# The first batch's 16-token blocks laid over each other, its zeros written by GpSimd, and the first chunk's PSUM pairs, layouts and conversion pieces put in another order

## The chip, the cores and the metric

The kernel runs on one core of a Trainium2 chip. The core has five engines that each work through a list of instructions in order and wait for one another by semaphores: TensorE (PE in the profile, its weight loads PEld), VectorE (DVE), ScalarE (ACT), GpSimd (POOL) and SyncE (SP), which here only starts transfers. The metric is the device time of one execution in microseconds (us); the median of several executions is compared.

## The reference

Two stages are chained. The first is a delta-rule recurrence over 768 tokens for 4 batches and 8 heads of width 48, the second a feed-forward layer with a slope `alpha` for negative values. All is float32.

```
k_n = k / (norm(k) + 1e-6)
for t in range(S):                                   # per batch b and head h
    y[t]  = q[t] @ state
    state = state + beta[t] * outer(k_n[t], v[t] - k_n[t] @ state)
x   = y as (3072 tokens, 384)                        # heads side by side
h   = x @ w_in                                       # 384 -> 2048
g   = max(h, 0) + alpha * min(h, 0)
out = g @ w_out                                      # 2048 -> 384
```

## The kernel before

**Tiling.** The tokens of a sequence are cut into 12 chunks of 64. One *step* is one chunk of two of the four batches, so there are 24 steps, numbered n. Within a chunk the recurrence is a triangular system of 64 x 64 per head: Gram matrices of the keys (`grams`) are weighted, the inverse of the triangle is needed (`inv`), and with it come `solve` (the corrected values u), `outputs` and `next_state`. Two steps of one chunk share 256 tokens, which then go through the feed-forward layer: `ffn_in` (48 matmuls of 128x256 for each chunk, each one two records in the profile) and `ffn_out`.

**Inverting.** VectorE does the inverse in batches of four steps. The diagonal blocks of 32 x 32 of the four steps and eight heads are put in the tile `same` (rows on the partitions). `turn_in` transposes them in 32 x 32 squares, four instructions of 128x256 (L567), into the tile `block`, where each partition owns a whole block. Then `eliminate` works on the free dimension, one multiply and one add for each column, and `back` transposes the result twice: into `turned` and into `inverse`, four instructions each.

The first batch (steps 0 to 3) has its own, shorter path, because everything waits for it: `eliminate_small` inverts only the two 16 x 16 blocks on the diagonal of each 32 x 32 block. It multiplies `block` by a mask `inside` (L626), runs 14 pairs of multiply (L632) and add (L638), and lets GpSimd write zeros and ones meanwhile (L643 to L645). The rest of the 64 x 64 triangle is then handled by iterating: `off_products` multiplies the inverted blocks, laid out by ScalarE (L675) and VectorE (L676) with the 0/1 columns of `which`, with the off-diagonal part `mid`, into `diag` (ScalarE, L689) and `away` (VectorE, L692); `substitute` (L727) and `substituted` (L734, L736) are applied three times for each of steps 0 and 1; then `place_inverse` (ScalarE, L741) builds `inv` for `solve` (L884). Steps 2 and 3 of the batch go the same way later, in `second_pair`, with `off_product` (L703: 32-row matmuls on `turned` itself) and `place_inverse`.

**Order.** All engines follow an order written out by hand (`manual_schedule`): an instruction is queued on its engine where the program issues it. The stretch around the change is: the Gram matrices of steps 0 to 3; filler matmuls (`busy`, L1575) while VectorE eliminates; `first_chunk` (steps 0 and 1); `second_pair` (steps 2 and 3), in which `alongside` mixes in a counted number of `ffn_in` matmuls (L1062) and of conversion steps; then long stretches woven from `ffn_in`, `ffn_out` and the attention of later steps, with numbers of feed-forward matmuls for each step given by `FILL` and `FILLS`. `first_chunk` also turns the keys of steps 4 to 6 (`flipped`, PE L430, ScalarE copy L439).

**Weights.** `w_in` comes in 12 pieces of 512 KB. Each is converted to the core's own form by ScalarE in two instructions (`begin_in(i)` runs as far as piece i: L262, L263) and by VectorE in two (`convert`, L272 and L277). The first eight pieces, and behind them the keys of steps 4 to 6 (`load_early`, L169), are requested by SP at the start.

**PSUM.** Three pairs of banks `p_pair` go round: `ps_big()` hands out the next one. Two more banks, `p_ffn`, are for the feed-forward layer.

## Time and profile before

| | |
|---|---|
| median of 3 executions | 636.96 us (636.45 to 640.7) |
| profiled execution: its time, its span | 637.52 us, 635.8 us |
| PE busy | 621.0 us of the span |
| VectorE, ScalarE, GpSimd busy | 502.4, 309.8, 98.4 us |
| VectorE starts turning the first batch | 15.36 us |
| first `substitute` done, flip of step 4's keys starts | 32.51 us, 32.55 us |
| first `ffn_in` matmul | 43.03 us |
| first `off_product` of `second_pair` (PE L703) | 46.62 us |

A line of the timeline gives the start of a group, the time from its first start to its last end, engine, line, operation, output and input, shapes and the number of instructions; in brackets stands how long the engine was idle before it, and what ended that. Consecutive instructions of an engine overlap a little at their ends, so that the distance between starts, not the duration, is what an instruction costs its engine in a row of independent ones. A matmul is two records. The `p_pair` number that an instruction uses isn't in these lines. Lines of the chain of waits give start, share of time and what it was spent on. Lines with stretches (`28.00:30.00`) give length, then busy time of PE, PEld, VectorE, ScalarE and GpSimd, the granted clock of TensorE, the busy share of the DMA engines, and GB/s.

### The profile page before, as it was taken

How to read it: one execution, taken by the hardware profiler on the slowest of the kernel's cores; microseconds unless marked ns; L12 is line 12 of the kernel's file. 1: busy time of each engine (PE TensorE's matmuls, PEld its weight loads, DVE VectorE, ACT ScalarE, POOL GpSimd, SP SyncE). 2: the span in 40 equal slices, each digit the busy share in tenths (PEclk: the TensorE clock that was granted, in tenths of full speed). 3: DMA queues.
4: the chain of work that ended last, by engine and by line, in shares of the span. 5: the costliest groups of instructions: out<-in, count | busy, mean ns of one | idle time of the engine just before them, and what ended most of it. 6: DMA issues, size and time to landing. Idle time of an engine off the chain costs nothing.

```text
span 635.8 us, 21637 instructions
## 1 busy us (share of the span) xinstructions
PE 621.0 (98%) x9116; PEld 548.8 (86%) x9116; DVE 502.4 (79%) x1219; ACT 309.8 (49%) x814; POOL 98.4 (15%) x214
## 2 busy tenths in 40 slices
PE   6889999999999999999999999999999999999997
PEld 5578887557788988989989989989999999999997
DVE  5888998978989988958978958878979579476383
ACT  6878465344553344645544636335347355353230
POOL 7021211010000000000000000000043052071350
PEclk9999999999999999999999999999999999999999
DMA  7968734211343242242242121211221300100000
GB/s 119 298 140 184 245 57 144 63 38 36 53 77 55 45 74 36 42 70 44 38 72 44 31 49 27 41 36 27 42 48 17 64 16 7 33 3 1 26 1 25
DMA packets 145968, 39.26 MB, mean 62 GB/s; under 512 B 139040, under 2 KB 142256, under 8 KB 145872
## 3 DMA queue, kind: packets, MB, share of 16 engines
q1 hardware_dynamic: 144000, 37.40, 28.8%
q8 instruction: 71, 1.16, 0.7%
q10 hardware_dynamic: 1872, 0.49, 0.4%
q14 instruction: 25, 0.20, 0.1%
HBM read 33.14 MB, written 4.72 MB: 60 GB/s over the span
## 4 chain that ended last, share of the span: by engine, by line
PE 82%; DVE 6%; ACT 2%; SPq 1%; issue 1%; DMA 1%; DVEq 0%; ACTq 0%
PE p_ffn L1062 14%; PE p_ffn L1126 9%; PE p_more L1396 8%; PE p_more L1126 8%; PE p_more L1062 7%; PE p_ffn L1105 6%; PE p_more L1312 4%; PE p_ffn L1302 3%; PE p_ffn L1396 3%; PE p_ffn L1307 3%; PE p_pair L859 2%; PE p_pair L790 2%; PE p_pair L897 2%; PE p_pair L884 2%; PE p_pair L841 1%; PE p_pair L502 1%
## 5 line engine op out<-in xcount | busy, mean ns | idle before, releaser
L1062 PE MATMUL p_ffn<-xt,w_in 128*128 128x256 f32 x528 | 123.5, 384 | 0.4 <-ACT space_out L263 0.2
L1062 PEld LDWEIGHTS p_ffn<-xt,w_in 128*128 128x128 f32 x528 | 97.6, 190 | 14.5 <-issue 0.9
L953 ACT COPY xt<-z 32x96 f32<-32x96 f32 x240 | 64.5, 269 | 49.0 <-DVE z L940 45.9
L1062 PE MATMUL p_more<-xt,w_in 128*128 128x256 f32 x240 | 55.7, 382 | 0.0
L1336 POOL TENSOR_TENSOR k_t<-k_t 128x128 f32<-128x128 f32 (+1 forms) x48 | 28.4, 592 | 166.3 <-ACT k_t L1331 163.8
L600 DVE TENSOR_TENSOR block<-block,prod 128x30 f32<-128x30 f32 (+9 forms) x150 | 49.9, 332 | 5.2
L1062 PEld LDWEIGHTS p_more<-xt,w_in 128*128 128x128 f32 x240 | 44.9, 190 | 6.3
L594 DVE TENSOR_TENSOR prod<-block 128x30 f32<-128x30 f32 (+9 forms) x150 | 48.5, 324 | 1.1
L802 ACT COPY inv<-p_pair 32x256 f32<-32x256 f32 x40 | 14.5, 363 | 71.6 <-DVE u L888 39.1
L419 POOL TENSOR_TENSOR beta_t<-beta_t,rec 128x8 f32<-128x8 f32 x24 | 6.6, 275 | 246.3 <-DVE rec L413 238.5
L1074 DVE SCALAR_TENSOR_TENSOR act<-act,al_t,p_ffn 128x256 f32<-128x256 f32 x72 | 31.0, 472 | 16.8 <-ACT act L1072 16.8
L1072 ACT ACTIVATE act<-p_ffn 128x512 f32<-128x512 f32 x36 | 21.4, 596 | 28.2 <-PE p_ffn L1062 27.9
L1336 POOL TENSOR_TENSOR block<-block 128x128 f32<-128x128 f32 (+1 forms) x48 | 28.0, 583 | 12.5 <-ACT block L1331 10.0
L1302 PE MATMUL p_ffn<-xt,w_in 128*128 128x256 f32 x96 | 29.3, 387 | 0.0
L1126 PE MATMUL p_ffn<-w_out,act 128*128 128x192 f32 x160 | 28.0, 327 | 0.6 <-DVE act L1074 0.6
L1126 PEld LDWEIGHTS p_ffn<-w_out,act 128*128 128x128 f32 x160 | 26.3, 190 | 1.1 <-DVE act L1074 0.9
L888 DVE TENSOR_TENSOR u<-p_pair,wgt 128x384 f32<-128x384 f32 x24 | 13.2, 553 | 17.6 <-PE p_pair L884 9.9
L1074 DVE SCALAR_TENSOR_TENSOR act<-act,al_t,p_more 128x256 f32<-128x256 f32 x40 | 17.3, 474 | 10.9 <-ACT act L1072 10.8
L869 DVE TENSOR_TENSOR r<-v_raw,p_pair 64x192 f32<-64x192 f32 (+1 forms) x66 | 23.2, 351 | 2.2 <-PE p_pair L859 1.2
L1126 PE MATMUL p_more<-w_out,act 128*128 128x192 f32 x128 | 22.3, 326 | 0.0
L1105 PE MATMUL p_ffn<-w_out,act 128*128 128x384 f32 x64 | 21.8, 491 | 0.4 <-DVE more L1074 0.4
L1331 ACT COPY k_t<-p_more 128x512 f32<-128x512 f32 x16 | 9.4, 587 | 25.8 <-PE p_more L1312 18.9
(275 smaller groups left out, 1479.0 us busy)
## 6 DMA issues: line engine op xcount, KB each, us to landing
w_out<-in_moe_w_in_dram SPq DMA_DIRECT2D x10, 512.0 KB, 5.6
v_raw<-in_v_dram SPq DMA_DIRECT2D x48, 96.0 KB, 2.7
kl<-in_k_dram SPq DMA_DIRECT2D x96, 48.0 KB, 2.4
out_dram<-o_sb SPq DMA_DIRECT2D x90, 48.0 KB, 1.6
space_out<-in_moe_w_out_dram SPq DMA_DIRECT2D x11, 384.0 KB, 4.3
ke_last<-in_k_dram SPq DMA_DIRECT2D x25, 96.0 KB, 3.2
qp<-in_q_dram SPq DMA_DIRECT2D x64, 32.0 KB, 2.2
w_out<-in_moe_w_out_dram SPq DMA_DIRECT2D x5, 384.0 KB, 4.4
```

What stands on the lines that cost most here:

```text
L594: nc.vector.tensor_tensor(out=prod, in0=r[:, 0:j, j : j + 1].to_broadcast([128, j, n]), in1=r[:, j : j + 1, j + 1 : HB].to_broadcast([128, ...
L600: nc.vector.tensor_tensor(out=r[:, 0:j, j + 1 : HB], in0=r[:, 0:j, j + 1 : HB], in1=prod, op=ALU.add)
L869: nc.vector.tensor_tensor(out=r[to, a], in0=v_in[to, a], in1=p[own, a, :, 0:D], op=ALU.subtract)
L953: nc.scalar.copy(to[quad(r), u, bp, t], z[quad(2 * t + u), r])
L1062: nc.tensor.matmul(p_h[:, i], w_in[:, t, (f + i) * 128 : (f + i + 1) * 128], xt[:, t], start=(t == 0), stop=(t == KT - 1),)
L1074: nc.vector.scalar_tensor_tensor(out=g[:, i], in0=g[:, i], scalar=al_t[:, f + i : f + i + 1], in1=p_h[:, i], op0=ALU.mult, op1=ALU.add,)
L1105: nc.tensor.matmul(p_o[u], gs[f // 2][:, f % 2, u * 128 : (u + 1) * 128], w_out[:, f], start=(f == 0), stop=(f == FT - 1),)
L1126: nc.tensor.matmul(p, x(i), w(i), start=(i == 0), stop=(i == FP - 1))
L1302: nc.tensor.matmul(p[:, f * 256 : f * 256 + 256], w(2, f), xt[:, 2], start=True, stop=False)
L1312: nc.tensor.matmul(q[:, j], a, b, start=True, stop=True)
L1336: nc.gpsimd.tensor_tensor(out=dst, in0=a, in1=b, op=ALU.add)
L1396: nc.tensor.matmul(p, x(i), w(i), start=(i == 0), stop=(i == FP - 1))
```

## The change

- `pack` is new: with a predicated copy, VectorE writes columns 16 to 31 of `same` over columns 0 to 15, on the rows that belong to the second 16-token block of each 32. It is done for steps 0 and 1 ahead of the last Gram weights, and for steps 2 and 3 behind them. `block` is then 32 x 16 for each 32 x 32 square, and `turn_in`, `turned` and `inverse` take two transposes each where they took four.
- The mask `inside` and its building (GpSimd memset and select, ScalarE cast L1772, VectorE multiply L626) are gone. `ends` has GpSimd write ones and zeros by nine memsets on `block`, which VectorE's transposes into `turned` wait for.
- `laid_out` spreads a 16-column result over four places by four 0/1 columns (`which_of`, built by VectorE at the start): the first `by_act` places by ScalarE, one instruction of 128x128 each, the others by one VectorE multiply. It stands for L675, L676 and L741. For steps 0 and 1, `inv` is built by ScalarE alone (eight instructions); for steps 2 and 3, VectorE builds `inv` and the matmul operand `inner`.
- `off_product` takes one step, with a pair of banks of its own: `own` in one half, `other` in the other, and `away` is copied for each step by itself. Steps 2 and 3 take it too, with 64-row matmuls on `inner` in place of L703. Calls of `ps_big()` alone shift which pair comes next; the flips of `first_chunk` then have a pair to themselves.
- The masks of `first_chunk` stand elsewhere, `begin_in` goes to 3, then 4, then 5 at three places in place of 5 and 6, the filler matmuls are shortened from 6 to 3.6 units of 512 columns behind the first two, the copies of `cross` and the scaling of `minus` come earlier on ScalarE.
- Much later, `FILL` for steps 13 and 14 is (12, 20, 10) and (12, 13, 9) in place of (12, 18, 12) and (12, 10, 12).

```diff
+    def halves_of(x):
+        return x.rearrange("p b c -> p (b c)")[:, 0 : NJ * H * LB].rearrange(
+            "p (b c) -> p b c", c=LB
+        )
+    def pack(first, last):
+        x = same[0][:, first:last].rearrange("p j h c -> p (j h) c")
+        lo, hi = x[:, :, 0:LB], x[:, :, LB:HB]
+        nc.vector.copy_predicated(
+            out=lo, mask=second_of.bitcast(U32)[:, 0:1, None].to_broadcast(list(lo.shape)), data=hi
+        )
...
         if (m, j) == (0, NJ - 1):
+            pack(2, NJ)
             for _ in turn_in(m):
                 pass
...
-        small[m] = own_blocks(flat)
+        wide = HB if m > 0 else LB
+        block[m] = flat[:, 0 : HB * wide].rearrange("p (r c) -> p r c", c=wide)
...
     def eliminate_small(m):
-        x = small[m]
-        nc.vector.tensor_tensor(out=x, in0=x, in1=own_blocks(inside_), op=ALU.mult)
-        yield
+        x = block[m].rearrange("p (s r) c -> p s r c", s=2)
+        ends(x)
...
-        yield from back(m)
+        turned[m] = halves_of(work.tile([128, NJ * H, HB], FP32, name="turned", bufs=1))
+        yield from turns(
+            lambda y: turned[m][:, :, y].rearrange("c (u b) r -> c r u b", u=2),
+            lambda y: x[:, :, y].rearrange("b s r c -> b r s c"), PIECES // 2,
+        )
+        inverse[m] = halves_of(work.tile([128, NJ * H, HB], FP32, name="inverse", bufs=1))
+        yield from turns(
+            lambda y: inverse[m][:, :, y].rearrange("r b c -> r c b"),
+            lambda y: block[m][:, :, y].rearrange("b r c -> b c r"), PIECES // 2,
+        )
+    def ends(x):
+        flat = x.rearrange("p s r c -> p s (r c)")
+        nc.gpsimd.memset(flat[:, :, :: LB + 1], 1.0)
+        nc.gpsimd.memset(flat[:, :, LB :: 2 * (LB + 1)], 0.0)
+        n = 2
+        while n < LB:
+            for at in range(0, LB, 2 * n):
+                nc.gpsimd.memset(x[:, :, at + n : at + 2 * n, at : at + n], 0.0)
+            n *= 2
...
+    def laid_out(to, src, n, by_act):
+        own = src[0][:, n * H : n * H + H]
+        to = to.rearrange("p b (q c) -> p b q c", c=LB)
+        for i in range(by_act):
+            nc.scalar.mul(to[:, :, i], own, which_of[:, i : i + 1])
+        if by_act < 4:
+            shape = [128, H, 4 - by_act, LB]
+            nc.vector.tensor_tensor(
+                out=to[:, :, by_act:], in0=own[:, :, None, :].to_broadcast(shape),
+                in1=which_of[:, None, by_act:, None].to_broadcast(shape), op=ALU.mult,
+            )
...
     def off_product(n):
+        p = ps_big()
+        own = p[:, 0, 0 : H * (C - LB)].rearrange("p (b i) -> p b i", b=H)
+        other = p[:, 1, 0 : G * (C - LB)].rearrange("p (b i) -> p b i", b=G)
         for b in range(H):
-            for i in range(4):
-                nc.tensor.matmul(
-                    p[quad(i), b], turned[0][quad(i), n * H + b], mid[n % 2][quad(i), b, LB:C]
-                )
-        nc.scalar.copy(diag[n % NE][:, :, LB:C], p)
+            for t in range(2):
+                w, y = inner(n)[half(t), b], mid[n % 2][half(t), b, LB:C]
+                nc.tensor.matmul(own[half(t), b], w, y)
+                if n < 2 and b >= G:
+                    nc.tensor.matmul(other[half(1 - t), b - G], w, y)
+        nc.scalar.copy(diag[n % NE][:, :, LB:C], own)
+        return lambda: nc.vector.tensor_copy(out=away[n][:, :, LB:C], in_=other)
...
-    def place_inverse(n):
-        for i in range(2):
-            nc.scalar.mul(... which[:, i : i + 1])
+    def place_inverse(n, by_act=0):
+        laid_out(inv[n % NE], inverse, n, by_act)
...
     def first_chunk(mask, inverted, convert):
-        aways = off_products(both)
         for i in both:
-            for _ in range(2 - i):
-                next(inverted)
-            aways[i]()
+            laid_out(inner(i), turned, i, 1 + i)
+        for i in both:
+            away_ = off_product(i)
+            next(inverted)
+            away_()
...
+                if (k, i) == (1, 0):
+                    mask(0, 1)
+                    place_inverse(0, 4)
                 if (k, i) == (0, 1):
-                    for j in both:
-                        place_inverse(j)
-                        place(j, (3,))
                     for j in (3, 2):
                         off_blocks(j, by_pool=True)
+                    begin_in(BEFORE + 1)
                 if (k, i) == (1, 1):
-                    begin_in(6)
+                    place_inverse(1, 4)
...
         now(solve(1))
+        begin_in(BEFORE + 2)
         convert(6)
...
-    busy(BUSY - 3.5, mid[1], p)
-    for _ in range(6):
-        busy(0.25, mid[1], p)
-    begin_in(5)
+    for _ in range(BUSY + 3):
+        busy(0.33, mid[1], p)
+    BEFORE = 3
+    begin_in(BEFORE)
...
     def second_pair():
         alongside(4, 1)
+        for i in both:
+            laid_out(inner(i), turned, i, 0)
         off_product(n)
...
+    FILL[13], FILL[14] = (12, 20, 10), (12, 13, 9)
```

## The prediction

> **What bounds the kernel now.** I read the busy shares first, then TensorE's waits, then the timeline of each engine from 14 to 62 us.
>
> ```profile
> PE 621.0 (98%) x9116; PEld 548.8 (86%) x9116; DVE 502.4 (79%) x1219; ACT 309.8 (49%) x814; POOL 98.4 (15%) x214
> ...
> 20.00:43.00 23.00, 19.52 (x492) 1.00 0.80 207
> 43.00:62.00 19.00, 18.91 (x443) 1.00 0.80 191
> 62.00:86.00 24.00, 24.00 (x488) 1.00 0.61 178
> ```
>
> TensorE is the bound: from 43 us it hardly idles, so what the change gains or loses up to there, and in the few waits that follow, moves the end one for one, provided that TensorE finds its operands ready afterwards. The changed stretch ends at 62 us. Before 43 us VectorE leads:
>
> ```profile
> 15.36 2.24 DVE L567 STREAM_TRANSPOSE block<-same 128x256 f32<-128x256 f32 x4 [0.21 <-ACT same L555]
> 17.63 0.69 DVE L626 TENSOR_TENSOR block<-block,inside 128x512 f32<-128x512 f32 x1
> ...
> 26.26 2.02 DVE L567 STREAM_TRANSPOSE turned<-block 128x256 f32<-128x256 f32 x4
> ...
> 40.41 0.42 DVE L272 TENSOR_SCALAR w_out<-w_out 128x512 uint32<-128x512 uint32 x1
> ...
> 49.58 0.87 DVE L1074 SCALAR_TENSOR_TENSOR act<-act,al_t,p_ffn 128x256 f32<-128x256 f32 x2
> ```
>
> **1. Up to the turned blocks.** From the first transpose to the first multiply of the elimination (18.36) is 3.00 us. The mask multiply goes, and two of four transposes (2.24 / 4 each). Added are two predicated copies, which no row shows. Bounds: the copy of 32x256 at 0.28 below, the 128x512 multiply at 0.69 above; I take the multiply of 128x256, 0.42, the same number of elements. The first stands ahead of the last Gram weights, where VectorE waits 0.19 for GpSimd, so it costs 0.22; the second costs 0.45 with its wait. So 0.22 + 0.45 + 1.15 = 1.82 in place of 3.00: 1.18 earlier. The 14 pairs keep their 7.9 us, and two transposes into `turned` save another 1.0: `turned` is whole at 26.1, not 28.3. The nine memsets cost GpSimd 0.15 to 0.31 each (its rows for 128x32 and 128x256), 1.4 to 2.8 us beside the 7.9; if they ran longer, VectorE's turns would wait. ScalarE's cast (1.04) went on while it had only to wait for VectorE. The added reductions at the start fall in VectorE's 3.41 us of idle time.
>
> **2. First products.** TensorE began 0.77 after the turned blocks (29.09). Now one ScalarE multiply of 128x128 (0.30 a piece, between the 32x128 copy and the 64x192 copy) stands beside a VectorE multiply of 384 elements (0.55, as L736): start at 26.8. A product takes 0.95 (96 records from 29.09 to 31.00). `away` of step 0 no longer waits for both products; it comes behind ScalarE's `diag` (0.48), so the first `substitute` is done near 29.5 against 32.51.
>
> **3. The keys hold it back.** The next thing in TensorE's order is the flip of step 4's keys:
>
> ```profile
> 19.11 1.83 SPq L169 DMA_DIRECT2D ke_pair<-in_k_dram  x2
> ...
> ke_pair<-in_k_dram SPq DMA_DIRECT2D x1, 96.0 KB, 11.7
> ...
> 26.00:28.00 2.00, 2.00 (x15) 1.69 (x13) 1.89 (x5) 1.94 (x5) 0.00 (x0) 1.00 1.05 361
> ...
> 32.55 0.65 PE L430 MATMUL p_pair<-ident,ke_pair 128*112 128x128 f32 x4
> ```
>
> The two transfers start at 19.11 and about 20.3 and land 11.7 and 10.8 us later, at 30.8 and 31.1: eight weight pieces run ahead of them, and the DMA engines are full. The change moves no transfer ahead of them. So the flip starts at 31.1, 1.45 earlier, not 3, and more than half of what VectorE saved is waited away. For the same reason the exact price of the predicated copy decides nothing: 1.5 us lie over it.
>
> **4. To `u` of step 1.** Before, 7.39 us passed from the flip's start to the start of VectorE's last `u` (39.94). In it, 1.06 is a wait of the last `substitute`, which shared a PSUM pair with ScalarE's copy of the flipped keys (start 36.99, copy's end 36.93), and it goes: the flips have a pair to themselves. Eight ScalarE layouts at 0.30 (2.4) replace four at 0.46, behind the conversion of piece 3 (1.35): `inv` of step 1 is ready at 36.5, about when it is asked for. I take 6.5 us: `u` starts at 37.6, 2.3 earlier. Bounds: 6.0 with no wait at all, 6.9 with layouts at 0.36.
>
> **5. First feed-forward matmul.** The conversion of piece 4 (1.35) now stands in ScalarE's queue before the copies of `y`; TensorE's transposes, `next_state` and `ffn_in` wait behind these. They start at 41.7, 1.3 earlier than 43.03. TensorE would reach `off_product` of step 2 at 46.62 - 1.3 = 45.3.
>
> **6. The new wait.**
>
> ```profile
> 46.62 0.88 PE L703 MATMUL p_pair<-mid,turned 32*32 32x48 f32 x64
> ...
> 59.00 2.48 PE L727 MATMUL p_pair<-r,diag 64*64 64x48 f32 x62
> ...
> 60.17 0.36 DVE r L869
> 60.53 0.04 issue
> 60.57 0.90 PE p_pair L727 x24
> ```
>
> L703 read `turned`, which had been there for 18 us. Now it reads `inner`, built by VectorE behind all the conversions and the first slope pair. VectorE works without a gap from 40.41 to 49.58 (9.17), and I find nothing taken out of that. So: 37.6, plus 0.47 for `u`, 9.17, 0.80 for the two slopes, 0.69 for one 128x512 layout (as L626) and 0.05 to TensorE: **48.8**. TensorE stands still from 45.3 to 48.8, 3.5 us, and is 2.2 later than before. Queued behind it are the flips, the second product and all the `ffn_in` matmuls of `second_pair`, though their operands are there.
>
> **7. From there to 62 us.** TensorE needed 12.38 from 46.62 to 59.00 without waiting. The two products have 32 records instead of 64, about 0.62 for 0.82: 11.98, so `substitute` of step 2 starts at 60.8, and both take 1.2: the Gram matmuls start at 62.0. Before, they started at 61.35, since `substitute` of step 3 waited 1.15 for `r`. ScalarE loses four L741 (1.84) from the chain to that `r`; 7.4 us after its slope activation (53.15 before, near 53.9 now) `r` is ready, at 61.3, as TensorE gets there. The VectorE layouts of `inv` (0.61 each) fall into its idle time of 1.73 before 53.77 and behind the masks of step 3; the second leaves 0.2 of 0.85 us of slack before `substitute` goes on at 64.85. Without this cover it costs up to 0.6.
>
> **8. FILL.** The numbers of steps 13 and 14 sum to 42 and 34 as before: no work. I put it at 0, within 0.3 either way for each step, the largest wait of the weight loads there.
>
> **Sum.** 62.0 - 61.35 = **+0.7 us**. On the profiled execution's own time (637.52, of it 635.8 span) that is 638.2; the median lies 0.56 lower, so I forecast **637.7 us**. Within 1% is about what can be told from no change here.
>
> **Rivals.**
>
> *A: TensorE's clock falls in the 3.5 us wait (slower).* This clock isn't what the column of the granted clock shows, which is 1.00 throughout:
>
> ```profile
> 19.48 3.33 PE L1575 MATMUL p_pair<-kl,ident 128*128 128x512 f32 x4
> 22.65 1.88 PE L1575 MATMUL p_pair<-mid,ident 128*128 128x512 f32 x4
> ```
>
> The same four records take 3.33 and then 1.88: TensorE was at half speed until about 22.2, after 2.7 us of dense filler. If it cools in the wait, 2.7 to 5.4 us of dense work go at half speed: 1.35 to 2.7 lost, 639.0 to 640.4. Against it: the wait of 1.08 before 29.09 left it at full speed, but no longer wait in a warm stretch is on record. It decides from a wait longer than that. The Trainium skill ("TensorE: Matmul & The Clock Gate", Part 1) says that the clock halves after an idle window of about 3.4 us, and that the windows run freely, so a wait just over one window need not contain one. The trace's warm-up agrees, at 2.7 us. By that page's figure two windows would be an estimated 6.8 us at half speed, 3.4 lost. Chance 0.2.
>
> *B: the layouts don't hold TensorE (faster).* If VectorE came to `inner` by 45.3, the 1.3 of part 5, 0.4 of the products and up to 1.15 of the wait for `r` would stay: 1.7 to 2.9 faster, 634.1 to 635.3. For it: the products of steps 2 and 3 are cheaper and ScalarE is relieved. Against: 9.17 us of conversions without idle time. Chance 0.12.
>
> *C: the keys land earlier, or `u` comes by 36.5.* Then the new wait shortens by 1.1 to 1.5: 636.2 to 636.6, as if nothing had changed. Against: the landing is set by 4 MB ahead in full queues. Chance 0.1.
>
> **Chances and range.** Forecast 0.55 (636.9 to 638.5 with the bounds of parts 4, 7 and 8), A 0.2, B 0.12, C 0.1, else 0.03. Leaving out the faster half of B, the end of A and the rest, the range is 634.5 to 640.6. Faster by over 1% (under 630.6) 0.02: no sum comes near. Slower by over 1% (over 643.3) 0.05: A lasting longer than any row shows. Same 0.93.
>
> **What will show it.** The flip of step 4 behind `substitute` on TensorE, waiting for the key transfer until about 31; the last `u` near 37.6; the products of step 2 waiting for VectorE's `sums` layout near 48.8, with TensorE idle for some 3.5 us before; the Gram matmuls at 62.0; matmuls of `ffn_in` at 0.22 a record behind the wait (0.43 if A holds). It is wrong if TensorE doesn't wait there, or if waits appear behind 62 us where before's list has none.

## The result and the profile after

The changed kernel takes 644.25 us (median of 6 executions, 642.15 to 647.11) beside 636.84 us for the kernel before (6 executions on the same chip, 636.14 to 640.7): a ratio of **1.0108, interval 1.0071 to 1.0145**. The forecast was 637.7 us with a range to 640.6. The profiled execution took 645.38 us with a span of 643.7 us; forecast on that basis was 638.2. Line numbers moved: L576 is the transposes, L543 `pack`, L703 `laid_out` on VectorE, L724 and L726 the products, L749 `substitute`, L905 `u`, L1079 `ffn_in`, L807 the 32x32 matmuls of `products` in the later steps, L1592 the idle filler.

The page's first line on TensorE, and the same three stretches as before (length, then busy time of TensorE's matmuls, its weight loads, VectorE, ScalarE and GpSimd, the granted clock, DMA share, GB/s):

```profile
PE 621.8 (97%) x9052; PEld 551.4 (86%) x9052; DVE 502.8 (78%) x1220; ACT 307.1 (48%) x814; POOL 95.8 (15%) x218
...
20.00:43.00 23.00, 19.29 (x529) 15.43 (x528) 18.21 (x49) 18.17 (x44) 4.80 (x8) 1.00 0.77 197
43.00:62.00 19.00, 15.02 (x233) 12.96 (x234) 11.60 (x26) 9.51 (x23) 1.54 (x4) 0.82 0.63 162
62.00:86.00 24.00, 23.23 (x502) 19.68 (x503) 21.30 (x53) 13.86 (x30) 5.02 (x12) 1.00 0.70 204
```

TensorE's busy time hardly grew, though 64 matmul and 64 weight-load records went. In the middle stretch it now idles 3.98 of 19 us, and the mean granted clock there is 0.82 where it was 1.00. VectorE's timeline:

```profile
13.43 0.42 DVE L543 COPY_PREDICATED same<-second_of,same 128x256 f32<-128x256 uint32 x1
...
15.21 0.44 DVE L543 COPY_PREDICATED same<-second_of,same 128x256 f32<-128x256 uint32 x1 [0.20 <-ACT same L563]
15.69 1.20 DVE L576 STREAM_TRANSPOSE block<-same 128x256 f32<-128x256 f32 x2
16.92 0.19 DVE L641 TENSOR_TENSOR prod<-block 128x28 f32<-128x28 f32 x1
...
24.82 1.06 DVE L576 STREAM_TRANSPOSE turned<-block 128x256 f32<-128x256 f32 x2
...
37.61 0.56 DVE L905 TENSOR_TENSOR u<-p_pair,wgt 128x384 f32<-128x384 f32 x1
38.08 0.42 DVE L271 TENSOR_SCALAR w_out<-w_out 128x512 uint32<-128x512 uint32 x1
...
48.04 1.28 DVE L703 TENSOR_TENSOR sums<-turned,which_of 128x512 f32<-128x512 f32 x2
```

The blocks are turned 2.4 us earlier than before, the last `u` of the first chunk starts at 37.61 instead of 39.94, and the layout `sums` comes behind the same conversions as forecast. TensorE's timeline and its longest waits:

```profile
31.23 0.62 PE L430 MATMUL p_pair<-ident,ke_pair 128*112 128x128 f32 x4 [1.75 <-DMA ke_pair<-in_k_dram]
...
41.22 1.13 PE L1079 MATMUL p_ffn<-xt,w_in 128*128 128x256 f32 x4
...
48.87 1.95 PE L724 MATMUL p_pair<-mid,sums 64*64 64x48 f32 x32 [3.98 <-DVE sums L703]
50.74 1.10 PE L430 MATMUL p_pair<-ident,ke_pair 128*112 128x128 f32 x4
...
63.77 0.43 PE L749 MATMUL p_pair<-r,diag 64*64 64x48 f32 x8
```

```profile
PE p_ffn L430 <- DMA ke_pair<-in_k_dram: 4.4, 1, 4.4
PE p_pair L724 <- DVE sums L703: 4.0, 1, 4.0
PE p_pair L807 <- issue: 2.0, 2, 1.4
PE p_pair L430 <- DMA ke_pair<-in_k_dram: 1.7, 1, 1.7
PE p_ffn L1079 <- ACT space_out L262: 1.0, 1, 1.0
...
PE p_pair L901 <- issue: 0.8, 1, 0.8
```

(In a line of the list of waits the numbers are the total, how often, the longest.) Two things here were not in the forecast. The flip behind the wait takes 1.10 us where the same four records took 0.62 at 31.23. And there are three stands put down to "issue", time in which TensorE waited for nothing that the profile shows; the kernel before had one of 0.33. Two more views of the changed kernel, stretches of 2 us around the wait, and the lines of the timeline with those stands:

```profile
46.00:48.00 2.00, 0.00 (x0) 0.00 (x0) 1.97 (x5) 0.00 (x0) 0.00 (x0) 0.73 0.96 265
48.00:50.00 2.00, 1.14 (x22) 1.17 (x23) 1.32 (x3) 0.00 (x0) 0.00 (x0) 0.50 0.70 115
50.00:52.00 2.00, 2.00 (x22) 1.91 (x20) 0.00 (x0) 0.48 (x1) 0.00 (x0) 0.50 0.75 145
52.00:54.00 2.00, 2.00 (x9) 1.70 (x8) 0.00 (x0) 1.26 (x3) 0.00 (x0) 0.56 0.93 357
54.00:56.00 2.00, 2.00 (x37) 1.59 (x36) 1.74 (x5) 1.94 (x6) 0.74 (x2) 1.00 0.38 98
```

```profile
80.81 0.49 PE L901 MATMUL p_pair<-v_raw,inv 64*64 64x48 f32 x18 [0.77 <-issue]
...
351.09 0.22 PE L807 MATMUL p_pair<-diag,right 32*32 32x32 f32 x2 [0.56 <-issue]
...
378.32 0.21 PE L807 MATMUL p_pair<-diag,right 32*32 32x32 f32 x1 [1.40 <-issue]
```

If a mean of 0.73 over 2 us is made of 1.00 and 0.50, the clock fell at 46.92; by the 0.56 it came back at 53.76. That is 6.84 us at half speed, of which TensorE had work in 4.89. TensorE went idle at 44.88 (48.87 less the 3.98 of the wait), so in this execution the clock fell 2.0 us into the idle time. The trace's own record of the clock has the same two moments, 46.93 and 53.76, and it shows more. In all 13 profiles of this case the times between two changes of the clock are multiples of 3.41 us, from 3.41 to 614.4, so the clock changed only at moments 3.41 us apart, which lie elsewhere in each profile. Below, a *slot* is the 3.41 us between two such moments. Here the slot that ended in the fall began at 43.52, with TensorE still at work, and was idle for 2.05 us.

To read the experiments I cut each profiled execution at two places that all kernels have: the first `ffn_in` matmul, and the first Gram matmul (L502 on TensorE) behind the two `substitute` calls of steps 2 and 3. In the kernel before they lie at 43.03 and 61.30, and 574.50 us follow; in the changed kernel at 41.22 and 65.56, and 578.14 follow. So the change gains 1.81 us up to `ffn_in`, loses 6.07 from there to the Gram matmuls, and 3.64 behind them.

### The profile page after: what moved, and what is told of

It is laid out like the page before. It is cut to its first block, busy times and chain, and to the rows that moved or that the text cites. A ratio compares the mean times of both kernels' runs of the same rounds, so it can differ in the third digit from the quotient of the medians.

```text
span 643.7 us, 21516 instructions
## 1 busy us (share of the span) xinstructions
PE 621.8 (97%) x9052; PEld 551.4 (86%) x9052; DVE 502.8 (78%) x1220; ACT 307.1 (48%) x814; POOL 95.8 (15%) x218
## 3 DMA queue, kind: packets, MB, share of 16 engines
q8 instruction: 71, 1.16, 0.7%
## 4 chain that ended last, share of the span: by engine, by line
PE 84%; DVE 7%; DMA 3%; ACT 2%; issue 1%; SPq 1%; ACTq 0%; DVEq 0%
PE p_ffn L1079 16%; PE p_ffn L1143 9%; PE p_more L1413 8%; PE p_more L1143 8%; PE p_more L1079 7%; PE p_ffn L1122 6%; PE p_more L1329 4%; PE p_ffn L1319 3%; PE p_ffn L1413 3%; PE p_pair L876 2%; PE p_ffn L1324 2%; DMA ke_pair<-in_k_dram 2%; PE p_pair L807 2%; PE p_pair L914 2%; PE p_pair L901 2%; PE p_pair L858 2%
## 5 line engine op out<-in xcount | busy, mean ns | idle before, releaser
L1079 PE MATMUL p_ffn<-xt,w_in 128*128 128x256 f32 x528 | 123.9, 385 | 1.1 <-ACT space_out L262 1.0
L1079 PEld LDWEIGHTS p_ffn<-xt,w_in 128*128 128x128 f32 x528 | 98.2, 191 | 15.1 <-ACT space_out L262 1.1
L1079 PE MATMUL p_more<-xt,w_in 128*128 128x256 f32 x240 | 55.7, 382 | 0.0
L1079 PEld LDWEIGHTS p_more<-xt,w_in 128*128 128x128 f32 x240 | 44.9, 190 | 6.3
L905 DVE TENSOR_TENSOR u<-p_pair,wgt 128x384 f32<-128x384 f32 x24 | 13.2, 553 | 19.6 <-PE p_pair L807 10.0
```

What stands on the lines that cost most here:

```text
L1079: nc.tensor.matmul(p_h[:, i], w_in[:, t, (f + i) * 128 : (f + i + 1) * 128], xt[:, t], start=(t == 0), stop=(t == KT - 1),)
```

## The experiments

The theories. **W**: the loss around 49 us is the wait for `sums` and the half-speed clock behind it. **M**, its rival: that stretch is slow for some other reason and would stay slow without the wait. **F**: the stands behind 66 us are TensorE's instructions arriving late. They come by a DMA queue of their own, 71 transfers of 16 KB for 18,104 matmul and weight-load records, 255 a transfer; the change took 128 of these records out of the products of steps 2 and 3, half a transfer, so that all later transfers end at other instructions. **V**, its rival: the new `FILL` numbers make these stands. The idle matmuls added below go into PSUM places that nobody reads; no kernel leaves work out.

**Layouts of steps 2 and 3 early.** They are issued in VectorE's idle time while TensorE waits for the keys.

```diff
                 if (k, i) == (0, 0):
                     mask(0, 0)
+                    for j in (2, 3):
+                        laid_out(inner(j), turned, j, 0)
...
     def second_pair():
-        for i in both:
-            laid_out(inner(i), turned, i, 0)
         off_product(n)
```

> The two VectorE layouts of steps 2 and 3 are issued in the first chunk, behind the first mask, where VectorE idled 2.1 us (30.4 to 32.5) for the keys; else the changed kernel. Theory W (the 4.3 us lost up to 66 us are the wait of the product of step 2 for that layout, 3.98 us, and the half-speed clock that follows it): no such wait, granted clock 1.00 from 46 to 54, the Gram matmuls that started at 65.7 start at 58.5 to 60, and 6 to 7 us go: 637.3 to 638.3 us. Theory M (the stretch is slow by something else, the layouts only show it): less than 2 us go, 642 or more. Theory F (3.6 us behind 66 us are lost because TensorE's instructions come in pieces of fixed size, and with 64 fewer records the piece ends fall in runs of small matmuls): TensorE's waits put down to issue, 0.8 and 2.0 us, stay, since its instructions are the same. Theory V (the new FILL numbers make them): they stay too.

Measured: 638.57 us, ratio to before 1.0013 (0.9998 to 1.0028), 0.3 us above the range expected by W. The wait is gone, the clock is 1.00 from 36 us on, and from `ffn_in` to the Gram matmuls pass 18.40 us in place of 24.34 (before: 18.27). M falls. The stands of F stay: 0.77, 0.16 and 1.12 us at 76, 345 and 372 us. And a second fall of the clock shows, in this execution, at the keys. Stretches of this kernel:

```profile
30.00:32.00 2.00, 0.63 (x4) 0.62 (x4) 1.67 (x4) 0.00 (x0) 1.90 (x4) 0.87 0.38 69
32.00:34.00 2.00, 2.00 (x66) 1.70 (x64) 0.52 (x1) 1.53 (x3) 1.90 (x3) 0.50 0.42 72
34.00:36.00 2.00, 2.00 (x77) 1.71 (x72) 1.15 (x5) 1.21 (x4) 0.63 (x3) 0.78 0.51 87
```

TensorE idled for 1.95 us there, from 29.42 to 31.37, the clock was down from 31.46 to 34.88, and `ffn_in` started at 42.62, 1.4 later than in the changed kernel. In the profiled execution of the changed kernel TensorE idled there for 1.75 us and the clock stayed. The lengths hardly differ; what differs is where the slots lie. Here all of the idle time falls in one, 28.05 to 31.46; there a moment at 29.87 cuts it into 0.4 and 1.37 us. Where the slots lie differs from profile to profile, so this is luck of the execution and not a difference between the kernels.

**Idle matmuls in the wait for `sums`.** Four matmuls of 128x512, then the product as it is.

```diff
         for i in both:
             laid_out(inner(i), turned, i, 0)
+        busy(4, mid[1], ffn_banks[(turn[0] + 1) % len(ffn_banks)])
         off_product(n)
```

> Four filler matmuls of 512 columns (3.4 us at full speed) stand before the product of step 2 and fill TensorE's wait; else the changed kernel. Theory W: the product still starts near 48.9, the clock stays at 1.00, the Gram matmuls start at 62.5 instead of 65.7, and about 3 us go: 641 us. Theory M, or a clock that costs nothing: 644 us as the changed kernel. Eight more TensorE records move the piece ends by 16 instructions, so by theory F the issue waits may change.

Measured: 640.2 us, ratio 1.0037 (1.002 to 1.0054). The timeline of TensorE in this kernel:

```profile
45.41 3.60 PE L1592 MATMUL p_ffn<-mid,ident 128*128 128x512 f32 x8
50.17 1.14 PE L724 MATMUL p_pair<-mid,sums 64*64 64x48 f32 x32 [1.16 <-DVE sums L703]
51.23 0.65 PE L430 MATMUL p_pair<-ident,ke_pair 128*112 128x128 f32 x4
```

The product still waits for `sums`, but behind it the flip takes 0.65 and not 1.10, the clock is 1.00 throughout from 44 to 60 us, and the product takes 1.14 and not 1.95. The edit also moved the ends of the transfers by 16 records, and there are no stands behind 66 us. So the time of this run does not separate clock and stands; a later run does. The clock's price can be read from the profile: from the start of this product to the Gram matmuls pass 14.43 us (50.17 to 64.60) in place of 16.69 (48.87 to 65.56), 2.26 less. The Gram matmuls come later than expected (62.5), since the product itself started 1.30 us later than in the changed kernel.

**The old `FILL` numbers in the changed kernel.**

```diff
-    FILL[13], FILL[14] = (12, 20, 10), (12, 13, 9)
```

> The FILL numbers of steps 13 and 14 are those of the kernel before; else the changed kernel. Theory V: the issue waits at 351 and 377 us (0.6 and 1.4) go, 642.2 us. Theory F: the one at 80 us stays and those at steps 13 and 14 move or change, since other work lies at the piece ends there; 642 to 645.5 us. Up to 66 us nothing changes.

Measured: 645.91 us, ratio 1.0138 (1.0108 to 1.0168). The stands are still there, 1.25 us at 349 and 1.57 at 376. V falls.

**128 records put back.** 32 idle matmuls of 64x48, that is 64 matmul and 64 weight-load records, in the wait for `sums`: behind them every instruction lies in its transfer where it does in the kernel before.

```diff
+        pad = ffn_banks[(turn[0] + 1) % len(ffn_banks)]
+        for _ in range(32):
+            nc.tensor.matmul(pad[0:64, 0:48], ident[0:64, 0:64], mid[1][0:64, 0, 0:48])
         off_product(n)
```

> 32 idle matmuls of 64x48 (64 records, the number that the change took out) stand before the product of step 2, in TensorE's wait, so that from there on TensorE has as many instructions behind it as in the kernel before; else the changed kernel. Theory F: the issue wait of 0.8 us at 80 us goes, and those at 351 and 377 us change; 0.8 to 2.8 us go, 641.4 to 643.4 us. Theory V: the waits at 351 and 377 stay, within 0.8 us of the changed kernel. By both, the wait for the layout and the half-speed clock stay, though the 0.6 us of matmuls may shift when the clock falls.

Measured: 643.31 us, ratio 1.0088 (1.0061 to 1.0116). No stands behind the Gram matmuls, and 574.99 us follow these: as in the kernel before (574.50), not as in the changed one (578.14). The median fell by less, because the profiled execution has stands of 1.05 and 0.68 us at 34.7 and 38.7, ahead of the edit, where the changed kernel's has none with the same instructions. The clock fell all the same. Stretches of this kernel:

```profile
47.00:49.00 2.00, 2.00 (x38) 2.00 (x37) 1.97 (x5) 0.00 (x0) 0.00 (x0) 1.00 0.83 149
49.00:51.00 2.00, 1.71 (x23) 1.57 (x22) 2.00 (x5) 0.00 (x0) 0.00 (x0) 0.54 0.75 119
51.00:53.00 2.00, 2.00 (x32) 1.91 (x30) 0.00 (x1) 0.47 (x1) 0.00 (x0) 0.50 0.87 264
```

From 45.89 to 50.26 TensorE's row is full of the idle matmuls, 64 records at 68 ns, all in one 64x64 corner of the array. They fill the slot that ended in the fall, 45.75 to 49.17, but for its first 0.14 us, and that was not enough to hold the clock; four 128-row matmuls of 512 columns in the run above were.

**Layouts early, and four idle matmuls ahead of the flip of step 4's keys.** This is the first run, with the wait for the keys kept busy as well.

```diff
+                if (k, i) == (0, 0):
+                    for _ in range(4):
+                        busy(0.33, mid[0], big[0][:, 1])
                 if i == 0 and k < 2:
                     now(flipped(NJ + k, ps_one()))
```

> The layouts of steps 2 and 3 early, as in the run with them moved, and four idle matmuls of 128x168 ahead of the flip of step 4's keys, into a half pair that nobody reads. In the run with the layouts moved TensorE stood 1.95 us for these keys (29.4 to 31.4 us), and the granted clock was 0.50 from about 31.5 to 34.9; in the changed kernel it stood 1.75 us and the clock stayed at 1.00. Theory W, extended to this wait (a stand of about 2 us drops the clock for 3.4 us, and that costs 1.5 us behind it): clock 1.00 from 28 to 60 us, the last u near 37.6 us, ffn_in near 41.2 us, about 0.8 to 1.5 us less than with the layouts moved alone, so 637.0 to 637.8. Theory F (the other stands come from where the 16 KB pieces of TensorE's instructions end, and 16 more instructions move the ends as in the run with idle matmuls in the wait for sums): no stands put down to issue at 80, 350 and 377 us, 2.1 us less: with both 635.3 to 636.5. If neither holds: 638.6 again.

Measured: 635.84 us (12 executions), **ratio to before 0.9975 (0.9961 to 0.9989)**: a version that beats the kernel before. Its timeline and two stretches:

```profile
29.64 1.41 PE L1592 MATMUL p_pair<-mid,ident 128*128 128x168 f32 x8
31.54 0.62 PE L430 MATMUL p_pair<-ident,ke_pair 128*112 128x128 f32 x4 [0.50 <-DMA ke_pair<-in_k_dram]
...
45.17 1.14 PE L724 MATMUL p_pair<-mid,sums 64*64 64x48 f32 x32
```

```profile
32.00:34.00 2.00, 2.00 (x86) 1.68 (x88) 1.16 (x4) 1.75 (x3) 1.86 (x4) 1.00 0.41 67
44.00:48.00 4.00, 4.00 (x50) 3.46 (x49) 3.97 (x10) 2.97 (x7) 0.00 (x0) 1.00 0.96 287
```

No half-speed clock and one stand of 0.41 us. The keys landed near 31.5 and held the flip there all the same.

**Layouts early, and the keys of step 4 asked for ahead of the weights.**

```diff
-    fetch_in(n_in)
...
     copy_1 = key(1)
+    load_early(1 + NKE)
+    fetch_in(n_in)
...
-    for n in range(1, NJ):
+    for n in range(2, NJ):
         load_early(n + NKE)
```

> The layouts of steps 2 and 3 early, and the two requests for step 4's keys ahead of the eight 512 KB requests for weights on SP's queue (issued near 15 us instead of 26.5), the weights' requests behind the flip of step 1's keys in the order of the program. Part 3 of the forecast (the keys hold the flip of step 4): the keys land near 20 us, TensorE's stand at 29.4 us goes, the last u is at 35.9 to 36.3 instead of 37.6, the clock stays at 1.00 from 28 to 60 us; VectorE's conversions, which are full from 38 to 47 us, begin up to 1.5 us earlier unless the weights, issued 1.3 us later, hold them. If TensorE sets the end from there: 635.5 to 637.1. If VectorE's conversions or the weights do: 638.6, as with the layouts moved alone. TensorE has as many instructions as in that run, so theory F expects stands at 80 and 350 to 380 us again, about 2 us together.

Measured: 638.54 us, ratio 1.0017 (1.0003 to 1.0031): nothing gained on the run with the layouts early (1.0013). The flip of step 4 starts at 30.00 without a wait, so the transfer was what held it. But the next flip, of step 5, then waits 1.09 us for its own keys; a stand of 0.43 follows, the clock is down from about 34.4 to 37.8, and `ffn_in` starts at 42.21.

**Half a transfer more in the kernel before.** 34 idle matmuls of 64x48 replace two wide ones near 25 us: 32 more matmuls, 128 more records, no other change. Behind 50 us the instructions lie in their transfers as in the changed kernel, which has 128 fewer.

```diff
-    busy(BUSY - 3.5, mid[1], p)
+    busy(BUSY - 5.5, mid[1], p)
+    for b in range(17):
+        for t in range(2):
+            nc.tensor.matmul(
+                p[half(t), 0:48], ident[half(t), half(t)], mid[1][half(t), b % H, 0:48]
+            )
```

> The kernel before, with 34 idle 64x48 matmuls in place of two of its idle 512-wide ones near 23 us: 128 more instructions on TensorE, half a 16 KB piece, so that behind 50 us the pieces end where they end in the changed kernel, which has 128 fewer; nothing else is changed. Theory F in its plain form (where the pieces end makes the stands): stands put down to issue near 80, 350 and 377 us, 2 to 4 us together, so 639.5 to 641. Rival (the stands come from what else the DMA engines and the queue do at that moment, in the changed kernel's order of transfers, not from the ends alone): no such stands, 637.0 to 638.0.

Measured: 642.36 us, ratio **1.0076 (1.0056 to 1.0095)**. The stands of its TensorE timeline (L790 and L897 here are L807 and L914 of the changed kernel):

```profile
41.56 0.45 PE L897 MATMUL p_pair<-u,a_t 64*64 64x48 f32 x16 [1.06 <-issue]
...
346.66 0.22 PE L790 MATMUL p_pair<-inv,mid 32*32 32x32 f32 x2 [1.20 <-issue]
...
375.46 0.25 PE L790 MATMUL p_pair<-diag,right 32*32 32x32 f32 x4 [1.72 <-issue]
```

A kernel that does the same work in the same order as the kernel before gets the stands at the 32x32 matmuls where the changed kernel has them, and 578.46 us behind the Gram matmuls, where the changed kernel has 578.14. The rival expectation (the changed order of transfers makes the stands) falls. The time is 1.4 us above the range expected by F. Two of the stands lie in slots that ended in a fall of the clock: it was at half speed from 43.36 to 46.78 behind the stand of 1.06 us, and from 347.15 to 350.56 behind that of 1.20. The expectation had neither, so part of what this run lost is the clock's.

The traces show the late delivery itself. They record when each 16 KB transfer of that queue is asked for and lands. In the 13 profiles there are 29 stands put down to issue behind 25 us, and at every one of them TensorE's next instruction starts 1.2 to 1.5 us after such a transfer has landed, and 2.2 to 2.9 us after it was asked for; in the changed kernel they land at 79.46, 349.66 and 377.00, and TensorE goes on at 80.81, 351.09 and 378.32. Stretches of 0.3 us behind each of 71 landings cover 3% of the span, so that isn't chance. The place fits as well: all 14 stands behind 340 us, in kernels with 128 or 112 records less than before and with 128 more, are 114 to 117 records behind a multiple of 256, counted from the first record.

**The `FILL` numbers alone, in the kernel before.**

```diff
+    FILL[13], FILL[14] = (12, 20, 10), (12, 13, 9)
```

> The kernel before with the change's last edit alone, the two new entries of FILL. Part 8 of the forecast (nothing, within 0.6 us): 636.9 to 638.1. Theory V, that the new entries cost what is lost behind 66 us: 639.5 to 641. The run of the changed kernel without them was 645.9, not less than 644, so V is not expected.

Measured: 638.16 us, ratio 1.0013 (1.0 to 1.0026), and 573.81 us behind the Gram matmuls, where the kernel before has 574.50. Nothing that can be told from noise, as forecast.

**The clock by itself.** Idle matmuls in the wait for `sums` again, and four fewer (wider) ones near 24 us, so that the ends of the transfers are those of the changed kernel.

```diff
-    for _ in range(BUSY + 3):
-        busy(0.33, mid[1], p)
+    for _ in range(BUSY - 1):
+        busy(0.5, mid[1], p)
...
+        busy(4, mid[1], ffn_banks[(turn[0] + 1) % len(ffn_banks)])
         off_product(n)
```

> The idle matmuls in the wait for sums again, but with four fewer (wider) idle matmuls near 24 us, so that behind 49 us TensorE's instructions have the same places in their 16 KB pieces as in the changed kernel: the clock's share by itself. Theory W: clock 1.00 from 40 to 60 us, stands put down to issue near 80, 350 and 377 us as in the changed kernel (2 to 3 us), 640.5 to 642, which is 2.5 to 3.5 us below the changed kernel and 0.5 to 1.5 above the run with idle matmuls alone. Rival (that run gained by the moved ends and not by the clock): 643.5 to 644.5.

Measured: 642.72 us, ratio 1.0065 (1.0037 to 1.0092); before on that chip 637.85. The median lies between the two expectations, and the interval overlaps that of the changed kernel, so the time alone decides little; the profile does. The stands are those of the changed kernel, almost to the hundredth (its TensorE timeline):

```profile
81.16 0.49 PE L901 MATMUL p_pair<-v_raw,inv 64*64 64x48 f32 x18 [0.72 <-issue]
...
350.56 0.22 PE L807 MATMUL p_pair<-diag,right 32*32 32x32 f32 x2 [0.55 <-issue]
...
377.80 0.21 PE L807 MATMUL p_pair<-diag,right 32*32 32x32 f32 x1 [1.41 <-issue]
```

The clock is 1.00 from 38 to 60 us, and from `ffn_in` to the Gram matmuls pass 22.69 us, the same as in the run with idle matmuls alone, beside 24.34. From the product's start to the Gram matmuls pass 14.43 us, as in that run. The edit had a price elsewhere: the idle matmuls near 24 us ended earlier, TensorE idled 2.71 us for the first products and 2.23 for the keys, and the clock was down from 32.42 to 35.84. Lines of its TensorE timeline and stretches around the two waits:

```profile
26.76 0.57 PE L724 MATMUL p_pair<-mid,act 64*64 64x48 f32 x13 [2.71 <-DVE act L703]
...
31.86 0.62 PE L430 MATMUL p_pair<-ident,ke_pair 128*112 128x128 f32 x4 [2.23 <-DMA ke_pair<-in_k_dram]
```

```profile
26.00:28.00 2.00, 1.24 (x59) 1.27 (x60) 1.47 (x4) 1.04 (x4) 0.00 (x0) 1.00 1.08 356
...
32.00:34.00 2.00, 2.00 (x64) 1.82 (x67) 0.42 (x1) 1.43 (x3) 1.94 (x3) 0.61 0.45 75
```

The longer gap left the clock at 1.00 and the shorter one brought it down: a moment at 25.60 cuts the longer one into 1.55 and 1.16 us, while all of the shorter one lies in one slot, 29.01 to 32.42. The fall came 2.8 us after TensorE went idle and 0.6 after it had gone back to work. Three of the six executions have a mean granted clock of 0.999 or 1.000; they took 641.63, 641.83 and 642.17 us.

**The best version with other ends.** Two variants of the run with both waits mended, the diffs against that run: of the narrow idle matmuls near 24 us, seven are replaced by 35 small ones (behind 50 us the ends are then those of the kernel before), or all eleven by seven wider ones (the ends of the changed kernel).

```diff
-    for _ in range(BUSY + 3):
+    for _ in range(BUSY - 4):
         busy(0.33, mid[1], p)
+    for b in range(35):
+        t = b % 2
+        nc.tensor.matmul(
+            p[half(t), 0:48], ident[half(t), half(t)], mid[1][half(t), b % H, 0:48]
+        )
```

> The layouts early and four idle matmuls ahead of the flip of step 4's keys, and near 24 us seven narrow idle matmuls replaced by 35 small ones, so that behind 32 us the instructions of TensorE have the places in their pieces that they have in the kernel before. Theory F: stands as in the kernel before (0.3 us near 39 us, none behind 60), 635.2 to 636.4, and the gain over before, 1 to 2 us, is the change's own with its two waits mended. If the gain of the run without the 35 was luck of the ends: 637 or above.

```diff
-    for _ in range(BUSY + 3):
-        busy(0.33, mid[1], p)
+    for _ in range(BUSY - 1):
+        busy(0.5, mid[1], p)
```

> The layouts early and four idle matmuls ahead of the flip, with four fewer (wider) idle matmuls near 24 us: behind 32 us the places in the pieces are those of the changed kernel, 16 instructions (1 KB) off those of the run without this edit. Theory F: stands near 80, 350 and 377 us again, 1.5 to 2.8 us together, 637.0 to 638.6. If 1 KB is too little to matter: 635.5 to 636.3.

Measured: 638.91 us, ratio 1.001 (0.9993 to 1.0026), for the first, and 638.8 us, 1.0005 (0.9985 to 1.0026), for the second. The first misses its expectation, and the expectation was drawn up wrongly: the 128 records that the change removed stood at 46 to 52 us, so only behind these are the ends those of the kernel before; from 25 to 46 us they are half a transfer off. There the stand turned up, and took the clock down for 3.4 us; behind the Gram matmuls there is none. The second lies 0.2 us above the range expected by F; the stand came back at one of three places. The stands of the two, each from its TensorE timeline:

```profile
37.40 0.26 PE L749 MATMUL p_pair<-r,act 64*64 64x48 f32 x2 [1.29 <-issue]
42.19 0.45 PE L914 MATMUL p_pair<-u,a_t 64*64 64x48 f32 x16 [0.35 <-issue]
```

```profile
369.78 0.21 PE L807 MATMUL p_pair<-diag,right 32*32 32x32 f32 x1 [1.35 <-issue]
```

So the 0.25% of the best version are what that kernel measured, but two neighbours that differ from it in idle matmuls alone are even with the kernel before. The runs don't divide this into its causes: the neighbours ran on another chip, and the clock took part, since 10 and 6 of their 12 and 10 executions have a mean granted clock of 0.997 or less, and one of 12 of the best version.

All profiled executions, one for each kernel, sorted by where the transfers end behind 50 us (records more or less than in the kernel before; 256 make a transfer, so +128 and -128 are the same place):

| kernel | records | `ffn_in` starts | to Gram matmuls | from there to the end | stands behind 66 us |
|---|---|---|---|---|---|
| before | 0 | 43.03 | 18.27 | 574.50 | none |
| `FILL` alone | 0 | 43.90 | 18.29 | 573.81 | none |
| 128 put back | 0 | 42.29 | 25.22 | 574.99 | none |
| both waits mended, 35 small | 0 | 44.36 | 18.02 | 574.62 | none |
| idle matmuls for `sums` | -112 | 41.91 | 22.69 | 574.80 | none |
| both waits mended | -112 | 41.56 | 18.04 | 575.00 | 0.41 |
| changed kernel | -128 | 41.22 | 24.34 | 578.14 | 2.73 |
| old `FILL` | -128 | 41.06 | 24.97 | 576.77 | 2.82 |
| layouts early | -128 | 42.62 | 18.40 | 576.48 | 2.05 |
| layouts and keys early | -128 | 42.21 | 18.02 | 576.57 | 1.37 |
| clock by itself | -128 | 43.26 | 22.69 | 577.15 | 2.68 |
| both waits mended, wider | -128 | 41.21 | 18.03 | 575.86 | 1.35 |
| before, 34 small | +128 | 43.93 | 19.61 | 578.46 | 2.92 |

The last two columns split by the second: all seven kernels whose transfers end half a transfer off have 1.35 us of stands or more and 575.86 us or more to the end, the six others 0.41 or less and 575.00 or less.

## Why the prediction was wrong

*Parts 1 to 6 held.* The copies took 0.42 and 0.44 (taken: 0.42), the first multiply started at 16.92 (17.18 by the sum), `turned` was whole at 25.88 (26.1), the first `substitute` ended at 29.49 (29.5), the keys held the flip until 31.23 (31.1), `u` started at 37.61 (37.6), `ffn_in` at 41.22 (41.7), and the product of step 2 at 48.87 (48.8) after 3.98 us of waiting (3.5). That the keys held the flip is shown by the run that asked for them earlier; that the wait for `sums` takes back what the first 41 us had gained, by the run with the layouts early (18.40 us to the Gram matmuls in place of 24.34).

Two steps failed: part 7, which had TensorE go on at full clock behind the wait, and the end of the sum, which put all that comes behind 62 us at nothing but for `FILL`.

*Part 7 failed*, by 3.56 us: Gram matmuls at 62.0 forecast, at 65.56 found (in the kernel before, the row has 61.30 and not 61.35). Three terms of its sum were too small.

- The step from 48.87 to `substitute` was put at 11.98 us; it took 14.90. With the clock up, in the best version, it takes 12.64 (45.17 to 57.81). So 2.26 us are the **half-speed clock**, which the forecast had only as rival A. The two runs that keep the wait but hold the clock give the same 2.26, up to the Gram matmuls.
- The other 0.66 are the products: 32 records of 64x48 were put at 0.62, less than the 0.82 of the 64 records that they replaced; they take 1.07 from start to start of the next row (45.17 to 46.24 in the best version), so the two products cost 0.90 more than forecast. The rest of the stretch ran 0.24 faster than before.
- Both `substitute` calls were put at 1.2 us; without any wait they take 1.79 (57.81 to 59.60). The wait for `r` in the kernel before was therefore worth 0.51 and not the 1.15 that the forecast handed back.

*Rival A* named the mechanism. Its chance of 0.2 was too low: all six executions of the changed kernel have a mean granted clock of 0.992 to 0.997. Its point of decision (a wait longer than 1.08 us) is not what the runs show, since a wait of 2.71 us left the clock up; what goes with the fall is how much idle time lies in one slot of 3.41 us. One sentence of it was wrong: the column of the granted clock does show the fall, 0.50. (The trace's record of the clock begins only at 22.23 in the kernel before, where the clock came up, and the column has 1.00 for what is ahead of that.) It put 2.7 to 5.4 us of dense work at half speed; 4.89 of the 6.84 us were such work, and 2.26 were lost. The Trainium skill ("TensorE: Matmul & The Clock Gate", Part 1), which the forecast cited for two windows of 3.4 us, or 6.8, agrees with this length, and with the 3.4 us after the keys. Its statement that the clock falls after an idle window of about 3.4 us is not what the runs show: the slots that ended in a fall were idle for only 2.05 us (the changed kernel) and 1.97 (layouts early) of their 3.41, and the measurement decides.

*Part 8 held as far as it went* (`FILL` is worth nothing by two runs), but the sum ended at 62 us, and 3.64 us more were lost behind the Gram matmuls: 2.73 in stands for instructions (shown by the run with 128 records put back, which has none of them and 574.99 us to the end, and by the run with 128 more in the kernel before, which gets them), 0.83 in a longer wait of `ffn_in` for ScalarE's converted weights near 108 us (1.02 in place of 0.19), which wasn't tried by itself. The forecast had a chance of 0.03 for all that it did not name, though its own last line called waits behind 62 us that the list of before lacks a sign of being wrong. The missing step was one line: the change takes 128 records off TensorE at 46 to 52 us, and every later 16 KB of instructions begins elsewhere. That a stand then comes could not be read from the profile before, but it could have been seen that its one stand (0.33 us, 39.43) stood within a run of small matmuls and that many such runs follow.

Together: 638.2 forecast, 2.26 for the clock, 0.66 and 0.59 for the two mis-sized rows, 0.07 for the product's start, 3.64 behind the Gram matmuls: 645.42, beside 645.38 measured.

*Rival B* did not happen: VectorE had no gap. With the layouts early it does, and then `ffn_in` to the Gram matmuls takes no longer than before, but the half clock at the keys and the stands took the gain. *Rival C* did not happen either, and the run that made the keys earlier shows that the next keys would have taken their place.

What stays open: which end of a transfer brings a stand, that is, which transfer comes too late. Of the three places at 80, 350 and 377 us, the changed kernel and the run with the clock by itself have all three to within 0.05 us, the best version with the same ends only the last; and two runs had stands of 0.4 to 1.1 us at 34 to 39 us, with the same instructions up to there as the changed kernel, which had none. What the DMA engines did at these moments was not varied.

## What to carry to other kernels

Ask of every new wait on the bounding engine not only how long it is but how long the engine then stays slow: here a wait of 3.98 us took 2.26 more behind it, and work that keeps the array wide (four 512-column matmuls), or operands laid out in an idle gap 18 us earlier, took that away. A gap that did no harm in one profile can do so in the next, when the clock's slots lie otherwise, so look at the mean granted clock of several executions. Where TensorE is full, a change in its number of instructions moves every later 16 KB of them, and runs of small matmuls at such an end can stand for up to 1.7 us; a kernel that is compared with its predecessor for less than 1% should be run with a few idle instructions more, to see how much of the difference is that. A gain early in the chain is to be followed to the next thing that does not move, here twice a transfer or a queue of conversions that stood where it was.

## What the runs showed of the hardware

- The granted clock changed only at moments 3.41 us apart, and behind 25 us it stayed at 0.50 for one or two such slots. In the 13 profiles it fell nine times there. Eight of the slots that ended in a fall had 1.20 to 2.95 us of idle time (2.05 in the changed kernel, 1.97 with the layouts early, 1.52 in two pieces with the keys early); the ninth is that with the small idle matmuls. Slots with up to 1.55 us of idle time ended without a fall, so between 1.2 and 1.55 something else decides; by the ninth case it may be the kind of matmuls, but that is not shown. Neither the length of a gap nor the time since it began does: the clock stayed up over gaps of 2.71 and 2.73 us that lay across two slots, and it fell 2.0, 2.8 and 2.95 us after TensorE went idle (changed kernel, clock by itself, old `FILL`).
- Each such 3.41 us takes 0.0027 off the mean granted clock of an execution of 640 us (half of 3.41 over 640). The six executions of the changed kernel have means of 0.992 to 0.997, one to three slots each by this estimate. All 29 executions of the kernel before beside the best version have 0.999 or 1.000, but 2 of 19 and 5 of 25 on the two other chips have 0.992 to 0.997.
- Busy is not always busy for the clock: 64 idle records of 64x48 in one corner of the array, 68 ns each and back to back for 4.37 us, did not hold it (it fell at 49.17, 3.3 us after they began); eight records of 128x512 did.
- TensorE's instructions come in transfers of 16 KB, and at some ends of them it stands for 0.2 to 1.7 us, in all 29 cases in runs of matmuls of 64 or 32 rows, until 1.2 to 1.5 us after a transfer has landed. Moving all ends by half a transfer cost 0.76% in a kernel that otherwise did the same, the half clock behind two of the stands included.
